# The last inverse transform with the state as the stationary operand, and x turned in place of the gated product

## The chip, the cores and the metric

The kernel runs on one core of one Trainium2 chip. A core has a matrix engine (TensorE, PE in the profile; PEld is its loading of the stationary operand), three engines for elementwise work (VectorE or DVE, ScalarE or ACT, GpSimd or POOL) and SyncE (SP), which here issues transfers. SBUF is the on-chip memory with 128 partitions; PSUM holds the results of matrix products in eight banks of 128 partitions by 512 fp32 numbers. The metric is the time of one launch in device microseconds (us); less is better.

A matrix product has a stationary operand (loaded first, PEld) and a moving operand (streamed through, PE). The result has a partition for each column of the stationary operand and a column for each column of the moving one.

## The reference

Everything is fp32.

```python
x, v: (4, 12480, 128)   pos_emb: (12480, 64)   w1: (64, 64)   w2: (64, 128)
h_filt = (maximum(pos_emb @ w1, 0) @ w2) * exp(-0.01 * pos)
u = x * v
y = irfft(rfft(u, n=2 * 12480, axis=1) * rfft(h_filt, n=2 * 12480, axis=0))[:, :12480]
z = x * y                                   # the gated product
h = z.reshape(49920, 128) @ moe_w_in        # (128, 2048)
out = (h * cos(h)) @ moe_w_out              # (2048, 128)
```

It is a long convolution along the sequence of each of 128 channels, a gate by x, and then a two-layer network over 49,920 tokens.

## The kernel before

**The convolution.** A sequence of 12,480 is seen as 104 (R) by 120 (N2), and the transform, over 2 x 96 x 120 points (N1 = 96), is made in stages of matrix products with tables of sines. The state of one batch lies in one large tile, `slots`: a partition, 64 channel pairs (`b`, CB), 240 places, and the two channels of a pair (`i`), so that neighbouring pairs stand 240 x 2 x 4 = 1920 bytes apart. The stages of a batch are u (u = x*v, and sums and differences of rows, into `slots`), f1, f2 (with the product by the filter's transform), i1 and i2. The 120 rows are taken four at a time (G = 4), two from the front and two mirrored, which makes NG = 30 groups in a batch. x and v come in by `load_pairs`, in pieces of 1024 bytes.

**i2, the last inverse step (L500 to L526, L670 to L693).** For each group there is a table `t` (name `tm`; 96 partitions, four rows, two terms, 104 columns). In batch 0 most of these tables are made on the spot and stored to `td`, afterwards they are loaded from there. Each of the four rows takes two products into a quarter of a PSUM bank: `t[:, i, r, :]` is stationary (104 columns), `slots[0:N1, :, place, :]` moves (128 channels). The result has 104 sequence positions on partitions and channels along the columns. `mm` (L129) cuts a product into two column halves of the array when `tiled` is set, as it is here. `i2_out` multiplies the bank by the x tile `xs` on DVE (L518) and stores the gated product to `zd` in DRAM (L522).

**The network.** Tokens go in NALL = 98 tiles of 128 rows of `zd`, that is 512 tokens. For each tile: `moe_load` (L734), then `moe_turn`, four transposes on PE into a bank (L742 through L136) and a copy to `at` on ACT (L744), so that channels lie on partitions. Then come 16 steps `c` (NFC), 128 hidden units each: `moe_up` (L751; the PSUM tile is `ph`), the cosine on ACT and DVE (L755, L756, L761, L762), sums on POOL (L770 to L774), and the second layer with seven products in place of eight (`moe_down`, L787, banks `acca`, `accb`). At the end of a tile `moe_evict` (L801 to L808), `moe_back` (four transposes into a `ph` bank, L813 to L818) and `moe_store` (L829).

**Order of the work.** The order on each engine is the program's; nothing reorders it at run time, and an instruction that waits holds up all that is behind it on its engine. SP issues nearly all transfers, in order. The first phase (to some 337 us) has no network work: it computes the filter (`filter_turn`, `filter_hidden`, `filter_out`; L871 to L892), takes the filter through f1, and in between makes the u tiles of batch 0 with `u_units(0, 3, ...)` (L862). This is a generator that is advanced two steps at a time from the fifth piece of the filter on, then one or two steps for each `filter_out`, and then one step for every two steps of f1. A group takes three such steps: two multiplies (POOL, some halves DVE, L404), then the sums (L410, one on POOL, one on DVE). With `bufs = 3` the pool has three `xt` and two `vt` buffers, and a group's loads (L398, L385) are issued one group ahead.

After that the network's steps run in a loop, and the convolution of the later batches is advanced beside them by the generators (`conv`): i2 of batch b with u of batch b + 1, then f1, f2 and i1. PSUM then has three `ph` banks, three banks (`cv`) that `bank()` hands out for the convolution and the turns, and one each for `acca` and `accb`.

## Time and profile before

| | |
|---|---|
| median of three runs | 3751.77 us (3749.74 to 3753.91) |
| the profiled execution | 3748.55 us, its span 3746.8 us |
| mean granted clock of TensorE | 0.994 |
| DMA over the span | 279.59 MB, mean 75 GB/s |
| DVE gate L518, mean | 681 ns |
| tile copies on ACT, L744 and L818 | 585 and 592 ns |
| u sums on POOL, L410, mean | 758 ns |
| POOL sums L482 and L774 | 739 and 733 ns |

The span is one execution as the hardware profiler saw it, from its first instruction to its last; the execution's own time is 1.75 us longer. A row such as "PE 3631.1 (97%) x40298" is an engine's busy time, its share of the span and its instructions. In a row of a group, "out<-in" gives the program's tile names, followed by shapes and a count; behind the first bar stand busy time in us and mean ns of one instruction, behind the second the idle time of the engine just before such instructions and what ended it. Rows of a time line begin with start and length in us; "x16" is a run of sixteen instructions. The chain is followed back from the last instruction, at each step to what released it.

### The profile page before, as it was taken

Reading aid. Unit: us, or ns where it says so; the run is one execution under the profiler, and the core shown is the slowest. Engines: PE = TensorE matmul, PEld = TensorE weight load, DVE = VectorE, ACT = ScalarE, POOL = GpSimd, SP = SyncE. Lnnn points to the kernel's source line nnn. Section 1 sums busy time; section 2 is a strip of 40 time slices with the busy share of each in tenths; the row PEclk is TensorE's granted clock in tenths of the full one; section 3 lists DMA queues with packets and bytes.
Section 4 is the critical chain, followed back from the end, with each engine's and each line's share of the span. In section 5 each row is a group of like instructions: output and inputs, shape, how many; then the busy total and the mean of one; then the engine's idle time right before and its main releaser. Section 6 shows DMA issues by size and latency. Waiting matters only on the chain.

```text
span 3746.8 us, 101339 instructions
## 1 busy us (share of the span) xinstructions
PE 3631.1 (97%) x40298; PEld 2592.9 (69%) x40298; DVE 2962.2 (79%) x5812; ACT 2252.4 (60%) x4660; POOL 2786.1 (74%) x3271
## 2 busy tenths in 40 slices
PE   7898999999999999999999999999999999999999
PEld 6777776766668776666667776766667776666666
DVE  7887887788887777788877777788887667777777
ACT  5756666655554556655555555665555446666666
POOL 6667887588874887588874788578884447887877
PEclk9999999999999999999999999999999999999999
DMA  6263551022212661022210553012220350000000
GB/s 167 66 185 100 163 155 49 20 65 72 73 43 58 169 163 45 18 69 73 66 40 21 157 163 99 15 53 73 67 70 13 107 147 21 21 19 24 18 24 14
DMA packets 209710, 279.59 MB, mean 75 GB/s; under 512 B 17112, under 2 KB 146536, under 8 KB 209112
## 3 DMA queue, kind: packets, MB, share of 16 engines
q1 hardware_dynamic: 209239, 273.12, 25.7%
q8 instruction: 320, 5.24, 0.6%
q14 instruction: 151, 1.23, 0.1%
HBM read 193.64 MB, written 79.42 MB: 73 GB/s over the span
## 4 chain that ended last, share of the span: by engine, by line
PE 79%; DVE 7%; POOL 2%; ACT 2%; issue 1%; DMA 0%; ACTq 0%; SPq 0%; POOLq 0%; DVEq 0%
PE ph L132 28%; PE cv L132 20%; PE accb L787 16%; PE acca L787 12%; DVE gt L762 2%; DVE gt L756 2%; PE cv L136 1%; ACT gt L755 1%; PE ph L136 1%; POOL ts L770 1%; DVE slots L431 0%; ACT tile L818 0%; POOL slots L410 0%; POOL ts L773 0%; DVE slots L433 0%
## 5 line engine op out<-in xcount | busy, mean ns | idle before, releaser
L755 ACT ACTIVATE gt<-ph 128x512 int32<-128x512 f32 (+1 forms) x1374 | 818.5, 596 | 1175.2 <-PE ph L132 1123.3
L756 DVE SCALAR_TENSOR_TENSOR gt<-ph,gt 128x512 f32<-128x512 f32 (+1 forms) x1374 | 944.3, 687 | 676.8 <-ACT gt L755 666.8
L770 POOL TENSOR_TENSOR ts<-gt 128x512 f32<-128x512 f32 (+2 forms) x784 | 1005.0, 1282 | 608.7 <-PE accb L787 542.1
L132 PE MATMUL ph<-at,w_in_sb 128*64 128x512 f32 (+1 forms) x5496 | 1428.6, 593 | 26.6 <-ACT tile L818 17.0
L761 ACT ACTIVATE gt<-gt 128x512 f32<-128x512 f32 (+1 forms) x1568 | 972.2, 620 | 4.2 <-DVE gt L756 3.4
L762 DVE TENSOR_TENSOR gt<-ph,gt 128x512 f32<-128x512 f32 (+1 forms) x1374 | 932.3, 679 | 0.0
L787 PE MATMUL accb<-ts,w_out_sb 128*64 128x128 f32 (+2 forms) x9408 | 652.2, 272 | 0.0
L774 POOL TENSOR_TENSOR ts<-gt,ts 128x256 f32<-128x256 f32 (+2 forms) x784 | 574.3, 733 | 61.5
L773 POOL TENSOR_TENSOR ts<-ts,gt 128x256 f32<-128x256 f32 (+2 forms) x784 | 573.0, 731 | 61.5
L787 PEld LDWEIGHTS acca<-gt,w_out_sb 128*64 128x64 f32 x6272 | 404.5, 137 | 239.1 <-issue 200.2
L787 PEld LDWEIGHTS accb<-ts,w_out_sb 128*64 128x64 f32 x9408 | 546.1, 137 | 0.0
L787 PE MATMUL acca<-gt,w_out_sb 128*64 128x128 f32 (+2 forms) x6272 | 482.9, 272 | 0.0
L787 PEld LDWEIGHTS accb<-gt,w_out_sb 128*64 128x64 f32 x3136 | 230.1, 137 | 254.8 <-issue 198.3
L132 PEld LDWEIGHTS ph<-at,w_in_sb 128*64 128x64 f32 x5496 | 354.9, 137 | 51.3 <-ACT tile L818 22.4
L482 POOL TENSOR_TENSOR slots<-slots,t 120x256 f32<-120x256 f32 x384 | 281.3, 739 | 125.8 <-DVE t L481 81.3
L132 PEld LDWEIGHTS cv<-slots,tm 96*64 96x64 f32 (+1 forms) x3840 | 246.6, 128 | 129.0 <-issue 118.3
L787 PE MATMUL accb<-gt,w_out_sb 128*64 128x128 f32 (+1 forms) x3136 | 313.6, 273 | 5.1 <-DVE ot L808 3.3
L787 PE MATMUL acca<-ts,w_out_sb 128*64 128x128 f32 (+1 forms) x3136 | 311.6, 272 | 2.3 <-POOL ts L773 2.3
L132 PE MATMUL cv<-slots,tm 96*64 96x128 f32 (+1 forms) x3840 | 278.7, 287 | 7.4 <-POOL tm L306 5.6
L132 PEld LDWEIGHTS cv<-cs,slots 120*64 120x64 f32 (+1 forms) x3072 | 167.3, 125 | 80.3 <-issue 70.9
L787 PEld LDWEIGHTS acca<-ts,w_out_sb 128*64 128x64 f32 x3136 | 204.8, 137 | 3.1 <-POOL ts L773 2.8
L132 PEld LDWEIGHTS cv<-c,slots 104*64 104x64 f32 (+1 forms) x1536 | 118.3, 137 | 114.6 <-issue 63.6
(145 smaller groups left out, 4134.9 us busy)
## 6 DMA issues: line engine op xcount, KB each, us to landing
h<-hd SPq DMA_DIRECT2D x144, 240.0 KB
tm<-td SPq DMA_DIRECT2D x96, 312.0 KB
xt<-in_x_dram SPq DMA_DIRECT2D x120, 208.0 KB
vt<-in_v_dram SPq DMA_DIRECT2D x120, 208.0 KB
xs<-in_x_dram SPq DMA_DIRECT2D x120, 208.0 KB
zd<-xs SPq DMA_DIRECT2D x119, 208.0 KB
tile<-zd SPq DMA_DIRECT2D x96, 256.0 KB
w<-wd SPq DMA_DIRECT2D x144, 116.2 KB
```

The costliest lines, as they stand in the source:

```text
L132: nc.tensor.matmul(dst[lo:hi], left[:, lo:hi], right, start=start, stop=stop)
L136: nc.tensor.transpose(dst, src, ident[0:n, 0:n])
L482: nc.gpsimd.tensor_tensor(y[:, r], y[:, r], t[:, r], op=op)
L755: nc.scalar.activation(turns, ph[:, 0:m], AF.Identity, bias=phase)
L756: nc.vector.scalar_tensor_tensor(out=part, in0=ph[:, 0:m], scalar=phase, in1=turns, op0=ALU.add, op1=ALU.subtract)
L761: nc.scalar.activation(part, part, AF.Sin, scale=scale)
L762: nc.vector.tensor_tensor(part, ph, part, op=ALU.mult)
L770: nc.gpsimd.tensor_tensor(ts[:, 0:2, 0:half], gt[:, :, half:2 * half], gt[:, 0, 0:2 * half].rearrange("p (h n) -> p h n", h=2), op=ALU.sub ...
L773: nc.gpsimd.tensor_tensor(t[2], t[1], b11, op=ALU.add)
L774: nc.gpsimd.tensor_tensor(t[3], b21, t[2], op=ALU.subtract)
L787: nc.tensor.matmul(acc[h * CB:(h + 1) * CB, place, 0:r], w_out_sb[:, pair, weight, :], right[:, h * r:(h + 1) * r], start=(pair == 0 and i ...
```

## The change

In i2 the operands change places: for each row, term and half h of a channel pair, `slots[0:N1, :, place, h]` (64 channels) is stationary and `t[:, i, r, :]` (104 columns) moves. The bank then holds channels on partitions, with the even channels on partitions 0 to 63 and the odd ones on 64 to 127, and 4 x 104 sequence positions as columns. To gate it, x is needed in the same layout. So x is turned: four transposes of a group's x tile (`x_turn`), a copy from PSUM by ACT (`x_keep`) back into the same tile, and a store from there to a new DRAM buffer `xd` (issued by ACT for batch 0, by SP later), from which i2 loads `xs`. The gated product goes to `zd` as [channel, row, token], and the network's tile is loaded straight into `at`; `moe_turn` and its copy are gone.

For batch 0 the turn of x is made in the first phase, in `u_units`: x is the tile `wt` there (two buffers), v is `ut` (three buffers). For batches 1 to 3 it is made in the network's steps: at c = 11 of each tile up to two x tiles are loaded (`x_load`), at c = 8 of the next they are turned (`x_next`), until all 120 groups are done. The channels of the state are taken in the order (n i b) instead of (n b i) when the filter and the u sums are written to `slots`, so the order of channels in a pair changes with it. `moe_back` takes its bank from the convolution's banks once batch 0 has gone through i2.

```diff
--- before.py
+++ after.py
@@ -111,7 +111,8 @@
 
     dram = ctx.enter_context(tc.tile_pool(name="dram", bufs=1, space=DRAM))
     hd = dram.tile([N1 // 2, N2, 2, CB, 4], F32, name="hd")
-    zd = dram.tile([NROWS, G, D], F32, name="zd")
+    zd = dram.tile([D, G, NROWS], F32, name="zd")
+    xd = dram.tile([B * NG, D, G * R], F32, name="xd")
     wd = dram.tile([N1 // 2, KE, 2, N2], F32, name="wd")
     td = dram.tile([N2 // G, N1, G, 2, R], F32, name="td")
     wind = dram.tile([D, DFF], F32, name="wind")
@@ -366,7 +367,7 @@
             nc.tensor.matmul(ps[0:FR, i * 2 * D:(i + 1) * 2 * D], aT[:, jj, 0:FR],
                              w2_sb[:, :], start=True, stop=True)
         above = pool.tile([FR, 2, CB, 2], F32, name="above", bufs=2)
-        pj = ps[0:FR, :].rearrange("p (n b i) -> p n b i", n=4, i=2)
+        pj = ps[0:FR, :].rearrange("p (n i b) -> p n b i", n=4, i=2)
         nc.scalar.copy(out=above[:, :, :, :], in_=pj[:, 2:4])
         a = H - 2 - 2 * j
         for place, op in ((a, ALU.add), (ODD + a, ALU.subtract)):
@@ -393,18 +394,28 @@
 
     def u_load(pool, bufs, b, a):
         tiles = []
-        for name, src, n in (("xt", x, bufs), ("vt", v, bufs - 1)):
-            t = pool.tile([R, 2, UA * D], F32, name=name, bufs=n)
-            load_pairs(t, src, b, H - UA - a, H + a)
+        for name, src, n in (("ut", x if b else v, bufs), ("wt", v if b else x, bufs - 1)):
+            t = pool.tile([P, 2, UA * D], F32, name=name, bufs=n)
+            load_pairs(t[0:R, :, :], src, b, H - UA - a, H + a)
             tiles.append(t)
         return tiles
 
     def u_multiply(tiles, half, engine):
-        xt, vt = tiles
-        engine.tensor_tensor(xt[:, half, :], xt[:, half, :], vt[:, half, :], op=ALU.mult)
+        ut, wt = (t[0:R, half, :] for t in tiles)
+        engine.tensor_tensor(ut, ut, wt, op=ALU.mult)
+
+    def x_turn(ps, t):
+        flat = t[0:R, :, :].rearrange("p h n -> p (h n)")
+        for i in range(G):
+            transpose(ps[:, i * R:(i + 1) * R], flat[:, i * D:(i + 1) * D], eye[0])
+
+    def x_keep(ps, t, b, g, queue):
+        there = t[:, :, :].rearrange("p h n -> p (h n)")[:, 0:G * R]
+        nc.scalar.copy(out=there, in_=ps[:, 0:G * R])
+        queue.dma_start(xd[b * NG + g, :, :], there)
 
     def u_sums(u, tiles, a, takers):
-        both = tiles[0][:, :, :].rearrange("p h (n b i) -> p h n b i", n=UA, i=2)
+        both = tiles[0][0:R, :, :].rearrange("p h (n i b) -> p h n b i", n=UA, i=2)
         below, above = both[:, 0, ::-1, :, :], both[:, 1, :, :, :]
         for place, op, e in ((a, ALU.add, takers[0]), (ODD + a, ALU.subtract, takers[1])):
             e.tensor_tensor(u[0:R, :, place:place + UA, :].transpose([0, 2, 1, 3]),
@@ -508,26 +519,28 @@
             else:
                 places = H + a, N2 + a
             for r, place in enumerate(places):
-                mm(ps[0:R, i * D:(i + 1) * D], t[:, i, r, :], slots[0:N1, :, place, :],
-                   start=(r == 0), stop=(r == 1))
-
-    def i2_out(pool, ps, xs, b, g):
+                for h in range(2):
+                    nc.tensor.matmul(ps[h * CB:(h + 1) * CB, i * R:(i + 1) * R],
+                                     slots[0:N1, :, place, h],
+                                     t[:, i, r, :], start=(r == 0), stop=(r == 1))
+
+    def i2_out(ps, xs, b, g):
         if b == 0:
             yield
-        flat = xs[:, :, :].rearrange("p h n -> p (h n)")
-        nc.vector.tensor_tensor(flat, ps[0:R, :], flat, op=ALU.mult)
-        z = xs[:, :, :].rearrange("p h (n d) -> p (h n) d", d=D)
         row = (b * NG + g) * R
+        z = xs
+        if row == 0:
+            z = ats[0] = mpool.tile([D, BANK], F32, name="at")
+        nc.vector.tensor_tensor(z[:, 0:G * R], ps[:, 0:G * R], xs[:, :], op=ALU.mult)
         if row > 0:
-            nc.sync.dma_start(zd[row:row + R, :, :], z)
-        else:
-            zbs[0] = z
+            nc.sync.dma_start(zd[:, :, row:row + R],
+                              xs[:, :].rearrange("p (g n) -> p g n", g=G))
         made[0] += 1
         yield
 
     rows_psum = []
-    made = [0]
-    zbs = {}
+    made, turned = [0], [0]
+    eye = []
 
 
 
@@ -564,7 +577,7 @@
     U_STEPS, F1_STEPS, F2_STEPS, I1_STEPS, I2_STEPS = 2.0, 0.8, 3.4, 0.8, 1.5
     FIRST_STEPS, I2U_STEPS = 3.5, 3.4
 
-    def u_units(b, bufs, u, engine, side="left"):
+    def u_units(b, bufs, u, engine, side="left", bank=None):
 
         with tc.tile_pool(name="xv", bufs=bufs, side=side) as pool:
             tiles = {}
@@ -572,16 +585,25 @@
             def before(j):
                 tiles[j] = u_load(pool, bufs, b, j * UA)
 
-            def after(j, _):
+            def mm(j, ps, i):
+                if b == 0:
+                    ps = bank()
+                    x_turn(ps, tiles[j][1])
+                return ps
+
+            def after(j, ps):
                 for half in range(2):
                     u_multiply(tiles[j], half, engine(j, half))
                     yield
+                if b == 0:
+                    x_keep(ps, tiles[j][1], b, NG - 1 - j, nc.scalar)
+                    turned[0] += 1
                 if j == H // UA - 2:
                     clear_gap(u)
                 u_sums(u, tiles.pop(j), j * UA, (nc.gpsimd, nc.gpsimd if b else nc.vector))
                 yield
 
-            yield from units(H // UA, U_STEPS, before, lambda j, ps, i: None, after, 3,
+            yield from units(H // UA, U_STEPS, before, mm, after, 3,
                              ahead=bufs - 2)
 
     def f1_units(bank, u, share=0.5, evict=f1_evict):
@@ -674,11 +696,13 @@
 
             def before(j):
                 ts[j] = pool.tile([N1, G, 2, R], F32, name="tm", bufs=bufs)
-                xss[j] = pool.tile([R, 2, UA * D], F32, name="xs", bufs=bufs + 1 + (b > 0))
+                xss[j] = pool.tile([D, G * R], F32, name="xs", bufs=bufs + 1 + (b > 0))
                 made_here = b == 0 and j not in SOME
                 if not made_here:
                     nc.sync.dma_start(ts[j][:, :, :, :], td[j, :, :, :, :])
-                load_pairs(xss[j], x, b, n2s(j)[0], n2s(j)[UA])
+                while turned[0] <= b * NG + j:
+                    x_ready()
+                nc.sync.dma_start(xss[j][:, :], xd[b * NG + j, :, :])
                 if made_here:
                     return make_group(pool, j, ts[j], 1)
 
@@ -689,7 +713,7 @@
                 return ps
 
             yield from units(NG, I2_STEPS, before, mm,
-                             lambda j, ps: i2_out(pool, ps, xss.pop(j), b, j),
+                             lambda j, ps: i2_out(ps, xss.pop(j), b, j),
                              4 if b == 0 else 2, ahead=bufs - 1, skip=int(b == 0))
 
     def inverse_units(bank, b):
@@ -730,19 +754,32 @@
 
     def moe_load(pool, n):
         m, row = rows_of(n), first_row(n)
-        zb = pool.tile([P, G, D], F32, name="tile", bufs=1)
-        nc.sync.dma_start(zb[0:m, :, :], zd[row:row + m, :, :])
-        zbs[n] = zb
-
-    def moe_turn(pool, n):
-        m = rows_of(n)
-        zb = zbs.pop(n)
-        pt = bank()
-        for i in range(G):
-            transpose(pt[:, i * m:(i + 1) * m], zb[0:m, i, :], ident)
         at = pool.tile([D, BANK], F32, name="at")
-        nc.scalar.copy(out=at[:, 0:G * m], in_=pt[:, 0:G * m])
+        nc.sync.dma_start(at[:, 0:G * m].rearrange("p (g n) -> p g n", g=G),
+                          zd[:, :, row:row + m])
         ats[n] = at
+
+    waiting = []
+
+    def x_load(pool):
+        job = turned[0] + len(waiting)
+        if job < B * NG:
+            t = pool.tile([P, 2, UA * D], F32, name="xw", bufs=2)
+            first, _, second, _ = n2s(job % NG)
+            load_pairs(t[0:R, :, :], x, job // NG, first, second)
+            waiting.append(t)
+
+    def x_next():
+        if waiting:
+            ps, t = bank(), waiting.pop(0)
+            x_turn(ps, t)
+            x_keep(ps, t, turned[0] // NG, turned[0] % NG, nc.sync)
+            turned[0] += 1
+
+    def x_ready():
+        if not waiting:
+            x_load(mpool)
+        x_next()
 
     def moe_up(pool, n, c, gt):
         m = G * rows_of(n)
@@ -810,7 +847,7 @@
 
     def moe_back(pool, n, ot):
         m = rows_of(n)
-        pt = ps_h.tile([P, BANK], F32, name="ph")
+        pt = ps_h.tile([P, BANK], F32, name="ph") if made[0] < NG else bank()
         places = pt[:, :].rearrange("p (h i e d) -> p h e i d", h=2, e=2, d=CB)
         for i, block in enumerate((1, 2, 3, 0)):
             transpose(places[0:m, i // 2, i % 2], ot[:, block, 0:m], ident)
@@ -846,8 +883,10 @@
 
 
             keep = tc.tile_pool(name="keep", bufs=1)
-            w2_sb = keep.__enter__().tile([P, 2 * D], F32, name="w2_sb")
+            kpool = keep.__enter__()
+            w2_sb = kpool.tile([P, 2 * D], F32, name="w2_sb")
             nc.gpsimd.memset(w2_sb[:, :], 0.0)
+            small = kpool.tile([P, R], F32, name="small")
             with tc.tile_pool(name="layers", bufs=1, side="right") as pool:
                 w1_sb = pool.tile([P, P], F32, name="w1_sb")
                 nc.gpsimd.memset(w1_sb[:, :], 0.0)
@@ -861,10 +900,12 @@
                     pes[i] = filter_load(pool, i)
                 first_u = u_units(0, 3, slots[0:R, :, :, :],
                                   lambda j, half: nc.vector if half and j % 3 and j < 18
-                                  else nc.gpsimd)
+                                  else nc.gpsimd, bank=bank)
                 next(first_u)
                 ident = pool.tile([P, P], F32, name="ident")
                 make_identity(nc, ident)
+                nc.gpsimd.tensor_copy(out=small[:, :], in_=ident[:, 0:R])
+                eye.append(small)
                 window = filter_window(pool)
                 nc.gpsimd.memset(aT[:, 0:H, NCH * ROWS:FR], 0.0)
                 sines = forward_tables(pool)
@@ -934,6 +975,7 @@
                 nc.sync.dma_start(here[:, :, :], kept[:, :, :])
             ident = wpool.tile([P, P], F32, name="ident")
             make_identity(nc, ident)
+            eye[0] = ident
             w_in_sb = wpool.tile([D, DFF], F32, name="w_in_sb")
             w_out_sb = wpool.tile([P, NFC // 2, 7, CB], F32, name="w_out_sb")
             nc.sync.dma_start(w_in_sb[:, :], wind[:, :])
@@ -983,7 +1025,6 @@
 
         while made[0] == 0:
             next(conv)
-        moe_turn(mpool, 0)
         steps = [(n, c) for n in range(NALL) for c in range(NFC)]
         hidden, pairs, gates, ots, obs = {}, {}, {}, {}, {}
         for i in range(len(steps) + LAG):
@@ -994,14 +1035,16 @@
                     ots[pn] = moe_evict(mpool, pn, pc % 2, ots.get(pn))
             if i < len(steps):
                 n, c = steps[i]
-                if n == 0 and c == NFC // 2:
-                    load(1)
-                if c == (NFC - 2 if n else NFC - 1) and n + 2 < NALL:
-                    load(n + 2)
-                if c == (NFC // 2 if n else NFC - 2) and n + 1 < NALL:
-                    moe_turn(mpool, n + 1)
-                if c == NFC // 2 and n - 1 in ots:
-                    obs[n - 1] = moe_back(mpool, n - 1, ots.pop(n - 1))
+                if c == (2 if n else NFC // 2) and n + 1 < NALL:
+                    load(n + 1)
+                if c == NFC // 2:
+                    for _ in range(2):
+                        x_next()
+                    if n - 1 in ots:
+                        obs[n - 1] = moe_back(mpool, n - 1, ots.pop(n - 1))
+                if c == NFC // 2 + 3:
+                    for _ in range(2):
+                        x_load(mpool)
                 if c % 2 == 0:
                     pairs[i] = mpool.tile([P, 2, BANK], F32, name="gt", bufs=4)
                 hidden[i] = moe_up(mpool, n, c, pairs[i - c % 2])
```

## The prediction

> **What bounds the kernel now.** I read the page from the top (busy times, slices, chain), then a table by stage, then short stretches in order of time and the groups with their shapes kept apart.
>
> ```profile
> span 3746.8 us, 101339 instructions
> ...
> PE 3631.1 (97%) x40298; PEld 2592.9 (69%) x40298; DVE 2962.2 (79%) x5812; ACT 2252.4 (60%) x4660; POOL 2786.1 (74%) x3271
> ...
> PE 79%; DVE 7%; POOL 2%; ACT 2%; issue 1%; DMA 0%; ACTq 0%; SPq 0%; POOLq 0%; DVEq 0%
> ```
>
> TensorE is busy 97% of the span and holds 79% of the chain; DMA holds none. So two things count: work taken from TensorE, and anything that makes it wait where it never waited. The table by stage (stretch, length, busy time of PE, PEld, DVE, ACT, POOL, granted clock, DMA share, GB/s) has the last inverse step of batches 1 and 2, then two windows of the first phase, which ends at 337 us:
>
> ```profile
> 1196.00:1430.00 234.00, 232.26 (x2832) 173.19 (x2828) 171.10 (x293) 124.80 (x229) 201.91 (x238) 1.00 0.58 159
> 2075.00:2300.00 225.00, 224.04 (x2746) 166.26 (x2744) 165.59 (x281) 119.38 (x218) 195.17 (x231) 1.00 0.60 164
> 60.00:70.00 10.00, 5.58 (x18) 5.61 (x19) 8.59 (x25) 2.42 (x10) 8.90 (x12) 0.53 0.62 178
> 80.00:90.00 10.00, 10.00 (x62) 9.79 (x61) 9.67 (x32) 9.16 (x41) 8.60 (x13) 1.00 0.56 160
> ```
>
> In the inverse step TensorE is full, POOL has 30 us to spare. In the first phase all four are near full; where TensorE idles (60 to 70 us) its granted clock falls to 0.53.
>
> **First phase: a chain through DRAM.** Today the 30 u tiles of batch 0 need no TensorE. By line, then in order of time:
>
> ```profile
> L404 POOL TENSOR_TENSOR xt<-xt,vt x48: 718/728/1507, 18.3 to 95.4; 104x256 f32<-104x256 f32 x48
> ...
> 80.94 0.36 SPq L385 DMA_DIRECT2D vt<-in_v_dram  x1
> 84.54 1.41 POOL L404 TENSOR_TENSOR xt<-xt,vt 104x256 f32<-104x256 f32 x2 [0.83 <-DMA vt<-in_v_dram]
> ```
>
> Thirty groups run from 18.3 to some 97 us, 2.7 each; a load takes 84.54 - 80.94 = 3.6 us from issue to use, and only POOL or DVE wait for it.
>
> The change puts four transposes of x (x_turn) per group on TensorE, which wait for the load of `wt`. `wt` has two buffers, and x_keep writes the turned x back into the same tile and stores it from there. So the load for group j+1 (on SP) waits until the xd store of group j-1 has landed; that store follows the copy of j-1 on ACT; in the changed program's order this copy stands behind `above` (L370) or an f1 eviction (L442, L443) whose products stand on TensorE behind x_turn(j). The loop: x_turn(j), a filter or f1 product, its ACT copy, the turned copy of j-1, the store, the load, x_turn(j+1). One group per turn of the loop, and all of TensorE's work behind x_turn, ACT's behind the copy, and the u load behind the `wt` load on SP stand still with it.
>
> Its terms: four transposes 0.50 (from 2501.07 to 2501.57 us at L742's place); one filter_out, four records at 10.00/48 = 0.21 (40 to 50 us), 0.83; L370 0.37; turned copy 0.51 (416 columns, L755); store 2.6; load 3.0; four hand-overs at 0.04 to 0.05 (queue rows of L366 and L370), 0.2. Together 8.0. In the f1 part six records at 10.00/62 = 0.16 and L442 + L443 (0.39 + 0.23) in place of filter_out and L370: 8.4. The transfers lie between these rows, the load also under the 3.6 above:
>
> ```profile
> 393.75 2.43 DMA vt<-in_v_dram
> ...
> SPq L734 <- DMA zd<-xs: 6.6, 2, 3.4
> ```
>
> The chain shows 2.43 us for a load of 208 KB; SP waits at longest 3.4 for a zd store (total, times, longest) that it issued just before. At 8.2 a group, 28 groups after the first two (which find free buffers) take 230 us; from 18.3 plus two of today's groups they end at 254 instead of 97: **+157**, as the order behind them is unchanged. With 2.4 for both transfers 7.4 a group, +134, and +100 if half the ACT and TensorE terms lie beside the transfers; with 3.4 and 3.6, and TensorE's 1.4 us doubled by a clock of 0.53, 11.0 a group, +235. I take 157: both transfers near the middle of their rows.
>
> **The product that is swapped (L511, after L521 to 524).** In order of time, group start to group start:
>
> ```profile
> 360.59 1.19 PE L132 MATMUL cv<-slots,tm 96*64 96x128 f32 x16
> 361.56 0.41 PE L787 MATMUL accb<-gt,w_out_sb 128*64 128x104 f32 x4
> 361.74 0.76 PE L787 MATMUL accb<-ts,w_out_sb 128*64 128x104 f32 x12
> 362.27 0.93 PE L132 MATMUL ph<-at,w_in_sb 128*64 128x416 f32 x4
> ...
> 2351.96 0.39 PE L787 MATMUL accb<-gt,w_out_sb 128*64 128x128 f32 x4
> 2352.18 0.82 PE L787 MATMUL accb<-ts,w_out_sb 128*64 128x128 f32 x12
> 2352.84 1.03 PE L132 MATMUL ph<-at,w_in_sb 128*64 128x512 f32 x4
> ```
>
> A product shows as four records (two halves, two passes). Four take 0.97 us in the inverse step, 0.2425 each, with 128 columns moving in pairs 1920 bytes apart; down products with 128 in a row take 0.88/4 = 0.22; with 104 in a row 0.53/3 = 0.177. There are 4 x 30 x 8 = 960 products. Afterwards 104 columns in a row move, and 64 single columns 1920 bytes apart are loaded per half. Loads wholly hidden: 960 x 0.0655 = 63 us gained. Their price in that form is in no row; the nearest:
>
> ```profile
> L132 PEld LDWEIGHTS cv<-slots,tm 96*64 96x64 f32 x1920 | 243.3, 138 | 107.0 <-issue 96.3 <-POOL tm L306 6.2 <-DVE tm L302 2.1
> L132 PEld LDWEIGHTS cv<-cs,slots 120*64 120x64 f32 x1536 | 167.1, 138 | 78.8 <-issue 69.5 <-ACT ot L801 4.7 <-DVE slots L496 4.2
> ```
>
> In a row (tm) or at 8-byte steps (slots), 64 columns load in 138 ns. But jumps of 1920 bytes cost the moving side 0.2425 - 0.22 = 0.0225 a product, 64 jumps per half and pass, as many as a load gets. Carried over: 0.177 + 0.0225 = 0.20, a gain of 960 x 0.0425 = **41**. The worst end, jumps at today's pace under nothing: 0.177 + 0.2425 = 0.42, 170 lost.
>
> [...] No row here shows single columns.
>
> **The turns.** Removed: 97 x four transposes of z (L742, 0.50) and an ACT copy (585 ns). Added behind the first phase: 90 turns of x, at 0.41 to 0.50. 48.5 - 42 = **-6**. The first phase's 15 us of transposes are in the loop above.
>
> **The output turn's bank.** The ph products idle 24.7 us, 17.0 of it on ACT L818, since L813 took one of three ph banks; after batch 0 it takes a conv bank. Between -24.7 and, where conv products in 45 tiles must wait 0.5 for two x turns and this one, +22: **-10**.
>
> **Rest.** x goes to xd and back: the 120 xs loads come from xd, 120 stores and 90 loads of some 208 KB are new, 44 MB on 280; tile becomes a load to `at`, in 512-byte pieces as the zd store. DMA share there is 0.58 to 0.60 and `at` is asked for 14 steps ahead; if late, a wait like the chain's 3.66 us for tm. SP's new waits (for the ACT copy, for TensorE's turn) hold up tm and u loads needed a group (8 us) later: **+3**. The gate falls from 681 ns (L518) to 579 (L762 at 416 columns), beside TensorE: 0. The u sums read pairs 256 bytes apart; POOL's only rows with steps (L482, 739) and without (L774, 735) agree: 0, at worst rival (4).
>
> Sum: 157 - 41 - 6 - 10 + 3 = +103. The profiled execution took 3748.55 (span 3746.8 and 1.75 around it): 3851.6. The median of the runs lies 3.2 higher, so I forecast 3855.
>
> **Rivals.**
> (1) Faster: the loop passes two groups at a time, since `wt` has two buffers. 4.1 a group, the groups end at 139, +42: 3740. It decides below (97 + 54 - 24)/28 = 4.5 a group. For it: the copy of j-1 needs nothing of x_turn(j) itself, only ACT's order binds them. Against: that order is fixed.
> (2) State loads are free: 63 instead of 41, ph waits go wholly, -15: 3818. For it: 138 = 138.
> (3) State loads bind, beside the 157: two halves of single jumps share the way, 0.28 a product: 960 x 0.0375 = 36 lost instead of 41 gained: 3932. It outweighs the rest of the gain from 0.2425 + 13/960 = 0.256. For it: the 0.0225 of today.
> (4) POOL binds: u sums half as long again (758 to 1137 ns): 195 + 60 x 0.38 = 218 us in the step of batch 2, about TensorE's 225 - 10. Two full engines waiting for each other lose some 10 in each of three such steps: 3885. For it: POOL's 195 of 225 already. [...]
>
> **How the numbers follow.** Forecast 0.42, (1) 0.08, (2) 0.15, (3) 0.22, (4) 0.13. A measurement can tell 0.2%, 7.5 us, from no change. Faster 0.07 (most of 1), same 0.02, slower 0.91. The range leaves out (1) and the upper half of (3): 3785 to 3930. All but (1) rest on the 157, so its bounds fill the range.
>
> **What would show it.** The first phase ends near 490 instead of 337, TensorE's share of it halves between 20 and 250 us, with its transposes (small, wt) waiting on the load of wt, starts 8.2 us apart. Wrong if they come under 4.5 apart, or if TensorE doesn't wait there. Four swapped products in 0.8 us (right), 0.71 (2), 1.0 or more (3). L410 on POOL at 758 or over 1000 ns, ph's idle time near 15 us.

## The result, and the profile after

The changed kernel takes 4001.33 us in the median of four runs (3990.91 to 4002.94), against 3751.4 before: a ratio of 1.066, interval 1.0641 to 1.0679. It is slower by some 250 us, where 103 were forecast. The profiled execution is the shortest of the four, 3990.91 us with a span of 3989.1, so the trace has to explain 242 us more span. Spans of profiled executions are compared below unless a text says otherwise; since this one is the lowest of its four, gains against it come out some 10 us smaller than gains between medians.

The page of the changed kernel: span, busy time of the engines, TensorE and its granted clock in 40 slices of some 100 us, shares of the chain.

```profile
span 3989.1 us, 102145 instructions
...
PE 3709.7 (93%) x40386; PEld 2635.1 (66%) x40386; DVE 2969.2 (74%) x5812; ACT 2264.2 (57%) x4682; POOL 2863.0 (72%) x3272
...
PE   4468989999999999999999999999999999999999
...
PEclk7669999999999999999999999999999999999999
...
PE 70%; POOL 7%; DVE 5%; ACT 2%; issue 2%; DMA 0%; ACTq 0%; SPq 0%; POOLq 0%; DVEq 0%
```

TensorE is 79 us busier and yet has a smaller share of the span. The first three slices, 300 us, are half empty at a clock of 0.6 to 0.7. POOL has gone from 2% to 7% of the chain. The copies of the network's output to SBUF (one for each of 98 tiles, L818 before and L855 after) mark the same work in both traces; their start times are

```
tile            0       20       30       45       60       97
before      398.7   1109.5   1514.6   2053.6   2599.9   3742.9
after       587.9   1336.3   1751.0   2309.0   2862.1   3985.3
later by      189      227      236      255      262      242
```

So 189 us are lost before the first tile, 66 more in tiles 0 to 45, which are those that turn x, 7 up to tile 60, and 20 come back in the tiles after it. TensorE's waits for the load of `wt` make up most of the first (total, times, longest):

```profile
PE ps L137 <- DMA wt<-in_x_dram: 137.1, 30, 6.2
```

The first phase as one window (columns as before: stretch, length, busy time of PE, PEld, DVE, ACT, POOL, granted clock, DMA share, GB/s), then one pass of the loop in order of time:

```profile
20.00:270.00 250.00, 118.66 (x377) 86.46 (x375) 60.81 (x171) 46.37 (x142) 65.86 (x73) 0.62 0.23 69
```

```profile
67.14 0.93 PE L137 MATMUL ps<-small,wt 104*128 104x104 f32 x4 [5.64 <-DMA wt<-in_x_dram]
...
67.86 3.62 PE L367 MATMUL ps<-w_sb,slots 128*96 128x256 f32 x8
69.82 0.37 ACT L371 COPY above<-ps 96x256 f32<-96x256 f32 x1 [7.15 <-PE ps L367]
...
71.57 0.37 ACT L371 COPY above<-ps 96x256 f32<-96x256 f32 x1 [1.38 <-PE ps L367]
...
72.03 0.51 ACT L414 COPY wt<-ps 128x416 f32<-128x416 f32 x1
...
72.56 0.34 ACTq L415 DMA_DIRECT2D xd<-wt  x1
...
74.62 0.31 SPq L386 DMA_DIRECT2D wt<-in_x_dram  x1
...
77.67 0.93 PE L137 MATMUL ps<-small,wt 104*128 104x104 f32 x4 [6.18 <-DMA wt<-in_x_dram]
```

This is the forecast loop link by link: turn, filter products, their copies, the turned copy (of the group before), the store, the load that waits for it, the next turn. No engine is busy half of the time in the window, and the granted clock is 0.62 over it, 0.50 between 67 and 72 us.

The swapped product, by groups and in order of time, and the u sums on POOL:

```profile
L523 PEld LDWEIGHTS cv<-tm,slots 96*64 96x64 f32 x3840 | 281.0, 216 | 114.6 <-issue 96.2 <-POOL tm L307 6.3 <-ACT gt L798 3.6
...
L421 POOL TENSOR_TENSOR slots<-ut 104x256 f32<-104x256 f32 x210 | 234.5, 1135 | 93.4 <-DVE ut L405 91.8
```

```profile
2363.64 1.14 PE L523 MATMUL cv<-tm,slots 96*64 96x104 f32 x16
2364.60 0.62 PE L824 MATMUL acca<-gt,w_out_sb 128*64 128x128 f32 x8
```

Four products take 2364.60 - 2363.64 = 0.96 us, as before (0.97), with 104 columns moving in place of 128: the loads have become longer (216 ns instead of 138). A POOL sum takes 1135 ns instead of 758. And in the list of waits (engine, what it waited for; total, times, longest) there is one that was not there before:

```profile
PE cv L137 <- ACT xw L414: 39.5, 66, 0.9
```

### The profile page after: what moved, and what is told of

Same layout as the page of the kernel before. It is cut to its first block, busy times and chain, and to the rows that moved or that the text cites. A ratio compares the mean times of both kernels' runs of the same rounds, so it can differ in the third digit from the quotient of the medians.

```text
span 3989.1 us, 102145 instructions
## 1 busy us (share of the span) xinstructions
PE 3709.7 (93%) x40386; PEld 2635.1 (66%) x40386; DVE 2969.2 (74%) x5812; ACT 2264.2 (57%) x4682; POOL 2863.0 (72%) x3272
## 4 chain that ended last, share of the span: by engine, by line
PE 70%; POOL 7%; DVE 5%; ACT 2%; issue 2%; DMA 0%; ACTq 0%; SPq 0%; POOLq 0%; DVEq 0%
PE ph L133 25%; PE accb L824 14%; PE cv L133 14%; PE acca L824 11%; PE cv L523 4%; POOL slots L421 2%; PE cv L137 2%; POOL ts L807 2%; DVE gt L793 1%; DVE gt L799 1%; POOL ts L810 1%; ACT gt L792 1%; ACT xw L414 1%; POOL ut L405 1%; POOL ts L811 1%
## 5 line engine op out<-in xcount | busy, mean ns | idle before, releaser
L133 PE MATMUL ph<-at,w_in_sb 128*64 128x512 f32 (+2 forms) x5504 | 1433.3, 595 | 5.4 <-DVE gt L799 5.0
L493 POOL TENSOR_TENSOR slots<-slots,t 120x256 f32<-120x256 f32 x384 | 281.8, 740 | 147.0 <-DVE t L492 99.5
L523 PEld LDWEIGHTS cv<-tm,slots 96*64 96x64 f32 x3840 | 281.0, 216 | 114.6 <-issue 96.2
L824 PE MATMUL acca<-ts,w_out_sb 128*64 128x128 f32 (+1 forms) x3136 | 312.0, 273 | 19.8 <-POOL ts L810 19.3
L421 POOL TENSOR_TENSOR slots<-ut 104x256 f32<-104x256 f32 x210 | 234.5, 1135 | 93.4 <-DVE ut L405 91.8
L523 PE MATMUL cv<-tm,slots 96*64 96x104 f32 x3840 | 273.4, 284 | 9.7 <-POOL tm L307 5.8
```

What stands on the lines that cost most here:

```text
L133: nc.tensor.matmul(dst[lo:hi], left[:, lo:hi], right, start=start, stop=stop)
L421: e.tensor_tensor(u[0:R, :, place:place + UA, :].transpose([0, 2, 1, 3]), below, above, op=op)
L493: nc.gpsimd.tensor_tensor(y[:, r], y[:, r], t[:, r], op=op)
L523: nc.tensor.matmul(ps[h * CB:(h + 1) * CB, i * R:(i + 1) * R], slots[0:N1, :, place, h], t[:, i, r, :], start=(r == 0), stop=(r == 1))
L824: nc.tensor.matmul(acc[h * CB:(h + 1) * CB, place, 0:r], w_out_sb[:, pair, weight, :], right[:, h * r:(h + 1) * r], start=(pair == 0 and i ...
```

## The experiments

Each edit is to the changed kernel unless it says otherwise. The median of the runs comes first, the profiled span in brackets. Where "less" or "later" has no other object, it is against the changed kernel.

**Where the loop of the first phase binds**

```diff
-        for name, src, n in (("ut", x if b else v, bufs), ("wt", v if b else x, bufs - 1)):
+        for name, src, n in (("ut", x if b else v, bufs - (b == 0)), ("wt", v if b else x, bufs - (b > 0))):
```

> The changed kernel with the third buffer of the first phase's pool given to the x tiles (wt 3, ut 2, instead of wt 2, ut 3); same room, same work. Loop theory (x_turn, product, copy, store, load, x_turn through one of two wt buffers): two groups pass per turn of the loop, so the turns come 4.5 to 6.5 us apart instead of 9.0 (6.5 where the ut tiles, now two, bind by load, multiplies and sums), the first phase ends 75 to 130 us sooner, and the run takes 3870 to 3925 us. Rival, that the first phase is long because TensorE has more work at a low clock or because the added transfers crowd each other: the turns stay 8.5 to 9.5 us apart, the run within 15 us of 3995.

Measured 3965.38 us (3964.9); the last turn starts at 249.3 us instead of 281.8, so the turns come 7.9 us apart instead of 9.0. The expected 4.5 to 6.5 was missed, and so were the rival's 8.5 to 9.5. The time line shows another way round:

```profile
60.70 0.93 PE L137 MATMUL ps<-small,wt 104*128 104x104 f32 x4 [5.90 <-DMA wt<-in_x_dram]
...
66.15 0.42 DVE L421 TENSOR_TENSOR slots<-ut 104x256 f32<-104x256 f32 x1
...
66.63 0.31 SPq L386 DMA_DIRECT2D ut<-in_v_dram  x1
...
67.11 0.33 SPq L386 DMA_DIRECT2D wt<-in_x_dram  x1
...
70.68 0.93 PE L137 MATMUL ps<-small,wt 104*128 104x104 f32 x4 [4.45 <-DMA wt<-in_x_dram]
```

The wt load no longer waits for a store, but it stands on SP behind the ut load, which follows a sum on DVE; that sum stands behind evictions of products that come after the turn. The store was only one way round; the order of the queues closes another. The edit takes from `ut` the buffer that it gives to `wt`, so part of the new way may be its own making; three buffers for both were not run.

Next the stores of the first phase are left out:

```diff
-        queue.dma_start(xd[b * NG + g, :, :], there)
+        if b > 0:
+            queue.dma_start(xd[b * NG + g, :, :], there)
...
-                nc.sync.dma_start(xss[j][:, :], xd[b * NG + j, :, :])
+                start = x[0, j * G * R:(j + 1) * G * R, :]
+                nc.sync.dma_start(xss[j][:, :], xd[b * NG + j, :, :] if b else bass.AP(
+                    tensor=start.tensor, offset=start.offset, ap=[[G * R, D], [1, G * R]]))
```

> The changed kernel without the 30 xd stores of the first phase; the xs tiles of batch 0 are loaded from x itself, in pieces of the same size, so batch 0 is gated by other numbers. The wt load then waits for the turned copy and not for a store. Loop theory: each turn of the loop loses the store's 2.06 us (trace of the changed kernel, 72.56 to 74.62) and no more, about 60 us over 28 groups: 3925 to 3945 us. Rival that the store is hidden behind other waits (the load, TensorE at half clock): within 15 us of 3995.

Measured 3935.89 us (3934.1), 55 less than the changed kernel's profiled execution, 65 less at the first tile. The turns come (220.7 - 19.4)/29 = 6.9 us apart, 2.1 less than before the edit: the store is in the loop with its full length of 2.06 us.

Then each turn is moved one group later in the program's order:

```diff
+            turns = {}
+
             def mm(j, ps, i):
-                if b == 0:
-                    ps = bank()
-                    x_turn(ps, tiles[j][1])
-                return ps
+                if b == 0 and j > 0:
+                    turns[j - 1] = bank()
+                    x_turn(turns[j - 1], tiles[j - 1][1])
...
-                    x_keep(ps, tiles[j][1], b, NG - 1 - j, nc.scalar)
+                    if j not in turns:
+                        turns[j] = bank()
+                        x_turn(turns[j], tiles[j][1])
+                    x_keep(turns.pop(j), tiles[j][1], b, NG - 1 - j, nc.scalar)
```

> The changed kernel with each first-phase turn of x put one group later in TensorE's order (the turn of group j - 1 where that of group j stood); buffers, loads and stores as changed. In wt_three the turns still came 7.9 us apart, since the ut load, ahead of the wt load on SP, waited for sums on DVE behind evictions whose products stand behind x_turn: any release that passes an engine's queue behind x_turn makes the loop. Here a turn finds its load landed, and the way from one turn to the load it frees spans two groups: 4.5 to 6 us a group, the first phase 85 to 125 us shorter, 3870 to 3910 us. Rival that the store and the load themselves (5.1 us) set the pace of a group: 8 us or more, above 3950.

Measured 3866.95 us (3862.9), 126 less and a little below the expected range, and the last turn at 153 us:

```profile
20.00:150.00 130.00, 87.13 (x396) 65.81 (x395) 67.47 (x182) 47.96 (x149) 69.43 (x77) 0.85 0.45 137
```

The turns come (153.0 - 19.9)/29 = 4.6 us apart, the granted clock is 0.85 instead of 0.62, and most turns' transposes take 0.55 us instead of 0.93. No transfer and no buffer was changed, only where TensorE's order has the turn. That settles the loop: of the 189 us at the first tile 133 go with it. The other 56 (tile 0 at 455.1 us against 398.7 before) stay, and were not taken apart.

**The swapped product and the sums**

```diff
-                                     slots[0:N1, :, place, h],
+                                     slots[0:N1, place % CB, 32 * h:32 * (h + 1), :].rearrange("p k i -> p (k i)"),
```

> The changed kernel with the stationary operand of the last inverse step taken from 64 state columns that lie in a row instead of 1920 bytes apart; the numbers are others, the count and size of all instructions the same. Theory that the single columns' loads set the product's pace: LDWEIGHTS of L523 falls from 219 to about 138 ns, four products from 0.96 to 0.71 to 0.80 us, and batch 3's step, where POOL has nothing to do, is 15 us shorter; the run 16 to 63 us shorter than 3995, nearer 16 if POOL holds the steps of batches 0 to 2. Rival that the moving side or the switch between halves sets 0.24: no change of the products.

Measured 4027.12 us (4027.5), slower by 38 where a gain was expected. This run is confounded: the places it reads are those into which the next batch's u sums write, and TensorE got a wait that it did not have (total idle ahead of L523, and what ended it):

```profile
L523 PEld LDWEIGHTS cv<-tm,slots 96*64 96x64 f32 x3840 | 207.1, 140 | 215.5 <-POOL slots L421 108.3 <-issue 89.5 <-POOL tm L307 6.3
```

Only batch 3's step, which has no u sums beside it, can be read from it: from its first swapped product to its last 116.5 us instead of 130.9. So the same was done with places that those sums do not write:

```diff
-                                     slots[0:N1, :, place, h],
+                                     slots[0:N1, place % CB, 128 + 32 * h:160 + 32 * h, :].rearrange("p k i -> p (k i)"),
```

> The changed kernel with the stationary operand of the last inverse step taken from 64 columns in a row, as in state_in_row, but from places 128 to 191 of a channel pair, which the next batch's u sums do not write (there TensorE's loads waited 108 us for those sums). Loads theory: four products 0.71 us, no new waits; 13.6 us gained in the step of batch 3 as there, 5 to 15 in each of the others (POOL has 203 of 214 us to do in batch 2's): 3935 to 3970. Rival that only the freed TensorE meets POOL: 3975 to 3985.

Measured 3976.0 us (3974.2), 15 less, as the rival expected. Products in order of time, their loads, the step of batch 2, and a wait (19.3 us in the changed kernel):

```profile
2363.69 0.89 PE L523 MATMUL cv<-tm,slots 96*64 96x104 f32 x16
2364.40 0.61 PE L824 MATMUL acca<-gt,w_out_sb 128*64 128x128 f32 x8
```

```profile
L523 PEld LDWEIGHTS cv<-tm,slots 96*64 96x64 f32 x3840 | 200.2, 139 | 134.9 <-issue 113.9 <-DMA tm<-td 6.6 <-POOL tm L307 6.3
```

```profile
2346.00:2560.00 214.00, 201.01 (x2608) 140.63 (x2604) 164.52 (x268) 110.29 (x201) 203.87 (x218) 1.00 0.61 164
```

```profile
PE acca L824 <- POOL ts L810: 37.1, 40, 2.2
```

Four products take 0.71 us, LDWEIGHTS 139 ns: the single columns were the price. But nearly all of the 15 us come from batch 3's step. In that of batch 2 TensorE now idles (busy 201 of 214 us) and POOL is as full as it (204).

The u sums in the old channel order:

```diff
-        pj = ps[0:FR, :].rearrange("p (n i b) -> p n b i", n=4, i=2)
+        pj = ps[0:FR, :].rearrange("p (n b i) -> p n b i", n=4, i=2)
...
-        both = tiles[0][0:R, :, :].rearrange("p h (n i b) -> p h n b i", n=UA, i=2)
+        both = tiles[0][0:R, :, :].rearrange("p h (n b i) -> p h n b i", n=UA, i=2)
```

> The changed kernel with the channel order of the kernel before (n b i) in the u sums and the filter's output, everything else as changed; the gate then meets other channels. Theory that the inner step of 256 bytes costs POOL its 50%: L421 falls from 1135 to about 758 ns. If POOL's 60 sums in the steps of batches 0 to 2 hold TensorE, the run gets 15 to 30 us shorter than 3995; if the state's loads hold it, the run stays within 10 us.

Measured 3972.66 us (3969.0), 20 less:

```profile
L421 POOL TENSOR_TENSOR slots<-ut 104x256 f32<-104x256 f32 x210 | 153.8, 750 | 96.5 <-DVE ut L405 94.7
```

Ten of the 20 us lie between tiles 50 and 55, where the u sums of batch 3 run on behind their step.

Both edits together, the second one of the state and that of the sums:

> The changed kernel with both edits, the state's columns in a row (state_in_row_2) and the u sums in the old order (sums_in_row); numbers differ, counts and sizes don't. Alone they gave 15 and 20 us by the traces (profiled span of the changed kernel 3989). Theory that in the steps of batches 0 to 2 each hides the other (the loads when POOL is full, POOL when the loads bind): together 60 to 80 us, a span of 3910 to 3930. If they only add: 3950 to 3958.

Measured 3915.57 us (3913.5), 76 less, where the two alone add to 35. Each had hidden the other. In the step of batch 2 TensorE is full again and POOL has room:

```profile
2300.00:2500.00 200.00, 199.08 (x2634) 142.11 (x2632) 167.42 (x267) 110.90 (x202) 181.62 (x218) 1.00 0.68 182
```

**The turns in the network's steps and the output turn's bank**

First all turns of batches 1 to 3 are left out, with their loads, copies and stores:

```diff
-                nc.sync.dma_start(xss[j][:, :], xd[b * NG + j, :, :])
+                start = x[b, j * G * R:(j + 1) * G * R, :]
+                nc.sync.dma_start(xss[j][:, :], xd[b * NG + j, :, :] if b == 0 else bass.AP(
+                    tensor=start.tensor, offset=start.offset, ap=[[G * R, D], [1, G * R]]))
...
     def x_ready():
-        if not waiting:
-            x_load(mpool)
-        x_next()
+        turned[0] += 1
...
-                    for _ in range(2):
-                        x_next()
...
-                if c == NFC // 2 + 3:
-                    for _ in range(2):
-                        x_load(mpool)
```

> The changed kernel without the 90 x turns of batches 1 to 3 (no xw loads, transposes, copies or stores; xs comes from x itself in pieces of the same size, so the gate meets other numbers). What goes is the whole price of the late turns: 90 x 0.41 = 37 us of transposes if they cost TensorE time alone (3955 to 3962); with the 40 us of waits for the copies as well, 70 to 90 us (3905 to 3925).

Measured 3912.13 us (3909.4), 80 less, all of it by tile 45. TensorE is busy 3662.3 us instead of 3709.7, so 47 us are work (0.53 us a turn) and 33 are waiting.

Next the two turns of a tile are set apart from each other and from the output turn:

```diff
+                if c in (4, 12):
+                    x_next()
                 if c == NFC // 2:
-                    for _ in range(2):
-                        x_next()
...
-                if c == NFC // 2 + 3:
-                    for _ in range(2):
-                        x_load(mpool)
+                if c in (7, 15):
+                    x_load(mpool)
```

> The changed kernel with the network's two x turns per tile taken apart: one at c = 4, one at c = 12, loads at c = 7 and 15, the output turn stays at c = 8. In the changed kernel tiles 0 to 45 (which turn x) take 1.5 us each longer than before, and TensorE waits 40 us in all for the turned copies on ACT. Bank theory (two x turns and the output turn ask for the three convolution banks at once): the waits go and the run is 25 to 50 us shorter than 3995. Rival that the turns cost what they take on TensorE and ACT wherever they stand: within 10 us of 3995.

Measured 3972.89 us (3970.4), 19 less: between the two theories, a part of both. Of the 39.5 us of waits for the turned copies next to nothing is left, but TensorE is 13 us busier (3722.5).

The output turn in a ph bank throughout, as in the kernel before:

```diff
-        pt = ps_h.tile([P, BANK], F32, name="ph") if made[0] < NG else bank()
+        pt = ps_h.tile([P, BANK], F32, name="ph")
```

> The changed kernel with the output turn always in a ph bank, as before; nothing else. Bank theory: the waits for the turned copies fall by more than half (from 40 us), but ph waits for ACT's output copy come back (17 to 25 us over the run): 3975 to 4000. Rival that the ph bank was worth its 25 us and the convolution's banks were free: 4010 to 4020.

The profiled execution took 3980.21 us (3978.4), 11 less. Of the two timed runs the other took 16,267 us, which resembles nothing else here and is left out; so this rests on one trace, and the four executions of the changed kernel alone lie 12 us apart. By its tiles it gains 20 us while x is turned and loses 9 after that. The waits for the turned copies fall from 39.5 to 22.3 us, a little less than the expected half, and ph waits of 9.4 us are back, where 17 to 25 were expected.

The change's own edit of the bank, put alone into the kernel before:

```diff
-        pt = ps_h.tile([P, BANK], F32, name="ph")
+        pt = ps_h.tile([P, BANK], F32, name="ph") if made[0] < NG else bank()
```

> The kernel before with one edit of the change: the output turn takes a convolution bank once batch 0 is through. The prediction's value for this term alone: 10 us gained (3741), between 25 gained and 22 lost. Bank theory, by tiles 60 to 97 of back_in_ph against the changed kernel (9 us lost without the edit where no x is turned): 5 to 15 us gained. Rival that moe_turn and the output turn crowd the convolution's banks: no gain.

Measured 3771.35 us (3768.9), a ratio of 1.0057 (1.0044 to 1.0071): 20 us slower, a loss that neither the theory nor its rival gave. From its list of waits:

```profile
PE cv L136 <- ACT at L744: 29.7, 44, 0.7
```

The 17.0 us of ph waits are gone, 29.7 us of waits for the copy of moe_turn's bank have come, and TensorE is 12 us busier (3643.0). To tell the bank from its neighbour, moe_turn was set at c = 4, with and without the edit:

```diff
-                if c == (NFC // 2 if n else NFC - 2) and n + 1 < NALL:
+                if c == (NFC // 4 if n else NFC - 2) and n + 1 < NALL:
                     moe_turn(mpool, n + 1)
```

> The kernel before with the output turn in a convolution bank once batch 0 is through, and moe_turn four steps ahead of it (c = 4 instead of 8), so that the two don't ask for convolution banks together. In before_new_bank, with both at c = 8, TensorE waited 29.7 us for moe_turn's copies and the run was 20.5 us longer. Neighbour theory (the bank itself is right, the two turns side by side are wrong): the 17 us of ph waits go without the 30 coming, 3735 to 3746. Rival that the convolution's three banks have no room for another taker at any place: 3757 to 3772.

> The kernel before with moe_turn at c = 4 instead of 8 and nothing else, the control of before_bank_apart: the output turn keeps its ph bank. Neighbour theory: the order of one turn alone changes nothing that binds, ph waits stay, 3747 to 3756. Rival that the early turn waits for its tile's load or crowds an earlier step: 3757 to 3775.

Measured 3764.78 us (3763.7) with the bank, 3787.63 (3785.9) without: both lie above what the theory of the neighbour gave, and the first falls into the range of its rival, that the convolution's banks have no room at any place. The pair speaks against that rival all the same: with moe_turn elsewhere the new bank gains 23 us, with moe_turn beside it, it loses 20. What had been overlooked is that setting moe_turn apart costs 37 by itself. TensorE's busy time in the run without the new bank shows most of that (3631.1 us before). Its ph waits grew too (17.0 before); with the new bank 1.4 us of them are left:

```profile
PE 3664.2 (97%) x40298; PEld 2572.3 (68%) x40298; DVE 2956.9 (78%) x5812; ACT 2263.2 (60%) x4660; POOL 2788.8 (74%) x3271
...
PE ph L132 <- ACT tile L818: 27.9, 39, 0.7
```

33 us more for the same instructions in 97 tiles are 0.34 us for each new place where transposes stand among the network's products. Added up group by group, TensorE's busy times do not rise (5440 us before, 5434 here); it is neighbouring groups that overlap less.

**Mended versions**

Both have the edits of the first-phase turns a group later (`turn_a_group_later`) and of the network's turns apart (`turns_apart`); the first, `mended`, has this one too:

```diff
-        pt = ps_h.tile([P, BANK], F32, name="ph") if made[0] < NG else bank()
+        pt = ps_h.tile([P, BANK], F32, name="ph") if turned[0] < B * NG else bank()
```

> The changed kernel, whole and with the reference's numbers, with the turn a group later, the two network turns apart (c = 4 and 12), and the output turn in a ph bank as long as x is being turned. If the three costs are independent: 85 to 125, 19 and 5 to 15 us, 3840 to 3885 us; still slower than before by 90 us or more, since the late turns' transposes and the sums remain and the swapped products gain nothing.

Measured 3861.66 us (3862.5): inside the expected range, but no gain in span over the later turn alone (3862.9), so the three costs do not add. In its waits ACT's output copy holds ph for 17.9 us again. The second, `changed_later_apart`, leaves the bank as changed:

> The changed kernel with the first-phase turns a group later and the network's turns apart, the output turn in the convolution's banks as changed: mended without its return to a ph bank. In mended ph waits for ACT's output copy came back (17.9 us), which may have eaten what turns_apart gained (18.7 us). If so: 3843 to 3852. Rival that turning apart is worth nothing once the first phase is shorter: 3862 to 3870.

Measured 3838.60 us (3837.0), a little below the expected range, the best of the changed kernels and 26 below the later turn alone. The two differ by the bank alone, 25.5 us in span: the return to ph was what ate the gain. It is still slower than before, by a ratio of 1.0233 (1.0214 to 1.0252). No version was found that beats the kernel before.

## Why the prediction was wrong

The sign, the place and the main mechanism were right; five terms were off in the same direction, and the time lies above the range. The largest misses are the swapped product (41 us) and the turns (39), then the first phase (32), the sums (20) and the bank (10).

**The first phase** (+157, measured +189). The loop is as predicted; turn_a_group_later and no_store show it. Store and load together were put too high (2.6 + 3.0, measured 2.06 + 3.05). What was too small is the work on TensorE: a turn 0.93 instead of 0.50, a filter_out (four records) 1.8 to 1.9 instead of 0.83 (3.62 for two in the pass shown), where the granted clock is 0.50 instead of 1.00. The prediction used a halved clock only for the upper bound. In some groups, as in the one shown, two filter_outs stand ahead of the turned copy where one was counted. The turns came 9.0 apart instead of 8.2, which over 28 groups is 24 of the 32 us; the other 8 were not traced.

**The swapped product** (-41, measured 0). The step that failed is "Carried over: 0.177 + 0.0225": a load of 64 single columns costs 216 ns against 138, and sets the product at 0.24. The runs show it: state_in_row_2 gives 0.71 for four products where the columns stand in a row, the changed kernel 0.96 where they stand alone. The value carried over came from the moving side; no row of before shows a load of columns 1920 bytes apart. The term was wrong a second time in that it took 960 products times a price as if no other engine were full: with loads of 139 ns the run gains 15 us as long as a u sum takes 1135 ns, and 56 (3969.0 to 3913.5) where it takes 750. Only that comes near the 63 of free loads.

**The turns** (-6). The 90 late turns cost 80 us, not 42: 0.53 us of TensorE each, and 33 us of waits. turns_apart points to two x turns and the output turn asking for three convolution banks in one step, each bank being freed by a copy on ACT: the 39.5 us of waits for these copies go with it. What leaving out moe_turn gave back was not measured by itself. The 242 less the 189, 80 and 20 leave some 47 gained, near the 48.5 predicted, but that remainder also holds the bank, the rest of +3 and whatever else was not measured. A second estimate: from tile 80 on, where the convolution is over, the changed kernel wins 6.5 us in 17 tiles, 0.38 a tile, which would make 37 in 97.

**The output turn's bank** (-10). Its price has both signs: 23 us gained with moe_turn elsewhere and again between mended and changed_later_apart, 20 lost with moe_turn beside it, about 11 lost in the changed kernel, where two x turns stand beside it (by one trace on each side). The prediction had the ends (-24.7 and +22) and chose by the wrong row: TensorE's idle time before the ph products did fall, to 4.3 us from 24.7, but the waits moved to the convolution's banks. Not how long ph waited, but who asks for the other banks in the same step decides.

**The sums on POOL** (0, measured +20). Rival (4) supposed 1137 ns, a time that no row of before shows, and +30; 1135 was measured, and 20 us. The row used, L482, reads runs of 16 bytes and says nothing of single elements. A u sum reading single elements took 1135/758 = 1.50 of one reading pairs.

So 189 + 80 + 20 - 47 = 242, which closes because the 47 are what is left over.

## What to carry to other kernels

When work is put on an engine that runs in order, follow the release of each buffer it reads through every queue it passes: if one of those queues stands behind the new instruction, the pass is a loop, and its length is paid once for each tile (9.0 us for each turn here). Moving the instruction one tile later in program order was worth more here (126 us) than another buffer (24). And a gain in one engine's time counts only as far as the next full engine (15 and 20 us alone, 76 together): test two suspected costs together, not only one by one.

## What the runs showed of the hardware

- Loading 64 stationary fp32 columns 1920 bytes apart took 216 ns, in a row 139 (state_in_row_2), at 8-byte steps 138 (the inverse step i1 in the kernel before, L132 on cs and slots). For the moving operand only a comparison of unlike products is at hand: four with pairs 1920 bytes apart took 0.97 us, four down products with columns in a row 0.88.
- Setting full-width transposes apart among column-split products cost TensorE 33 us in 97 tiles with one new place in each (before_turn_early, 0.34 a place) and 13 us in 45 tiles with two (turns_apart, 0.14 a place). So turns side by side were cheaper in TensorE's time than turns apart, but not by a fixed price. No run shows the reason.
- TensorE waiting for a DMA in every group was granted 0.62 of its clock over 250 us, 0.85 over 130 us where the turns came 4.6 us apart instead of 9.0.
- A sum of 104x256 fp32 elements on POOL took 1135 ns reading single elements 256 bytes apart, 750 reading pairs (sums_in_row).
